# Sums stored tile by tile, and routing steps moved, in a fused attention and two-layer mixture-of-experts kernel

## The chip, the cores and the metric

The kernel runs on one core of one Trainium2 chip. Its engines are TensorE (PE: matmuls; PEld: its weight loads), VectorE (DVE), ScalarE (ACT), GpSimd (POOL) and SyncE (SP), with 16 DMA engines that move data between the chip's main memory (DRAM) and the core's on-chip memory (SBUF); PE writes its sums to PSUM. The metric is the device time of one execution in microseconds (us), as the median of three runs.

## The reference

Attention of 4 batches, 8 heads, 576 positions, 64 dimensions, in two steps over 32 packed queries, gives 2304 tokens of 512 numbers. A first mixture of experts takes all 4 experts for every token, weighted with given probabilities. A second takes, for every token, the two experts with the largest noisy logits out of 8:

```python
def _moe2_ref(x, w_gate, w_noise, noise, w1, w2):
    logits = x @ w_gate
    noise_scale = np.log1p(np.exp(x @ w_noise))
    noisy_logits = logits + noise_scale * noise
    top2 = np.argpartition(-noisy_logits, 2, axis=1)[:, :2]
    top2_l = np.take_along_axis(noisy_logits, top2, axis=1)
    top2_l = top2_l - top2_l.max(-1, keepdims=True)
    top2_w = np.exp(top2_l)
    top2_w /= top2_w.sum(-1, keepdims=True) + 1e-09
    out = np.zeros((N, D), dtype=np.float32)
    for e in range(E):
        for k in range(2):
            mask = top2[:, k] == e
            ...
            h = np.maximum(x[mask] @ w1[e], 0.0)
            out[mask] += top2_w[mask, k, None] * (h @ w2[e])
    return out.astype(np.float32)
```

N is 2304, D 512, F (the hidden width) 1024, and all numbers are float32.

## The kernel before

**Matmuls.** A float32 product is made of three matmuls of numbers split into a high and a low half (`mm3`, L64 to L67: high·high at L65, high·low and low·high at L66 and L67). The halves are made on arrival by ACT (high, L70) and by DVE or POOL (low, L71); for hidden values by L476 (ACT) and L477 (DVE).

**Stages.** Attention comes first, then the first mixture (MoE1), whose second matmul for the last block runs tile by tile (128 tokens each), five tiles of eight steps; places in this stretch are written `TM + 8*t + f` with TM = 200. Then comes the second mixture (MoE2); its places are `S2 + 8*j + f` with S2 = 300, where j counts blocks of work and f the eight steps of one.

**Blocks of MoE2.** An expert has room for 640 tokens, five tiles. The blocks in order are: tiles 0 to 2 of expert 0, tiles 0 to 2 of expert 1, tiles 3 and 4 of expert 0, tiles 3 and 4 of expert 1 (`EA` = 2 early experts, `tA` = 3 early tiles), and then experts 2 to 7 with all five tiles. A block is `e_mm1` (first matmul, hidden values to `gh`, `gl`) one step ahead of `e_mm2` (second matmul, sums in `acc`), and at the end of its last step `y_out` (L887, L889) writes each tile, times its weight, to `Y`.

**Routing.** Tokens are routed in four groups of tiles (`Route`): `ra` tiles 0 to 8, `rb` 9 to 12, `rc` 13 to 15, `rd` 16 and 17. `r1` (L548) stores a tile of x to `x2d` in DRAM and transposes it. `pos1` counts ranks with small matmuls of `utri` and `ones` (L628, L630, L633), `pos2` (DVE) makes the slots, `put` (L682, POOL) writes one record of 16 bytes per token and choice to `meta` in DRAM by an indirect DMA, `rest` (L701, L702) stores `sdd` and `gwd` for a fallback.

**Records and rows.** `mt_early` (L746) loads the records of the three early tiles of experts 0 and 1; `mt_index` (L759) casts them to integers `mti`, on POOL for the early ones. For the experts from 2 on (`mt_rest`, called in `mt_late`) it also runs 32 small matmuls on PE (L766) and makes an index `iq` of quarter rows (L768, DVE). `gather` fetches the rows `xg` of x from `x2d` (L811 whole rows for experts 0 and 1, L820 quarter rows for the others), `xg_t` turns them (L833 on PE for experts 0 and 1, by DVE for the others).

**Sums over the two experts of a token.** A token's lower expert leaves its part in `yd` in DRAM: `y_store` (L906) stores all five tiles of `Y[e]`, 1280 KB, once per expert, at the place `s + 8.13` of the block of work that ends it. `g_load` (L847) gathers the parts of earlier experts from `yd` into `gt` on POOL, after `g_zero` (L843, a memset). `y_out` or `y_add` (L894) adds them and `y_scatter` (L898, POOL) writes rows to the output; each row is written in the end by the token's higher expert.

**What sets the order.** Every engine works through its instructions in program order, and SP and POOL their DMA issues too. The order is written by hand: `at(place, f)` puts a step into a list, and `run(upto)`, called after every tile of matmuls, carries out the steps whose place has been reached, in the order of places. The weights (`raw`, 512 KB each, L132) are issued by SP in the same order, in three buffers; a load waits until its buffer has been split.

Of the kernel before, what the change touches and what calls it, by code (L numbers as in the profile page):

```python
# [15 lines left out]
OP = mybir.AluOpType  # L16
# [4 lines left out]
D, FF, E1, E2 = 512, 1024, 4, 8  # L21
# [9 lines left out]
def tile_pack_attn_moe_moe(ctx: ExitStack, tc: tile.TileContext, qT, kT, pT, vv, dp, noise,  # L31
                           w1, w2, m1, m2, wg, out, cap=CAP):
    nc = tc.nc
# [25 lines left out]
    yd = tc.dram_tile((NSLOT, D), F32, name="yd")  # L59
# [23 lines left out]
    cnt = consts.tile([128, 8], F32, name="cnt")  # L83
# [61 lines left out]
    def at(place, f, *a):  # L145
        fill.append((place, len(fill), f, a))
# [7 lines left out]
    TM, S2 = 200, 300  # L154
# [11 lines left out]
    for k in range(8):  # L166
        e = k % E1
# [6 lines left out]
    tA = T2 - T2 // 2  # L174

    EA = 2
    subs = [(e, 0, tA) for e in range(EA)] + [(e, tA, T2 - tA) for e in range(EA)] + [(e, 0, T2) for e in range(EA, E2)]
    vec, gps = nc.vector, nc.gpsimd
# [283 lines left out]
    for n, u in enumerate(at_u):  # L462
        s = 15 + 18 * n
# [4 lines left out]
        s = (50, 58)[n]  # L468
# [245 lines left out]
    ra, rb, rc, rd = Route(0, 9, aux_ps), Route(9, 4, acc_ps), Route(13, 3, mm_ps), Route(16, 2, mm_ps)  # L714
# [6 lines left out]
    for t in range(4):  # L721
        at(120.14 + t, rb.r1, t)
        at(121.13 + t, rb.r2, t)
    rb.tail([125.2, 126.1, 126.2, 127.1, 127.2, TM + 8.5, TM + 9.5], (TM + 10.2, 0.01))
    at(TM + 10.5, lambda: nc.vector.tensor_scalar(cnt[:, 0:EA], cnt[:, 0:EA], float(tA * 128), None, op0=OP.max))
    at(TM + 8, rc.begin)
    for t in range(3):
        at(TM + 8 * t + 9.4, rc.r1, t)
# [10 lines left out]
    XG, XT, Gt, H2, Y = {}, {}, {}, {}, {}  # L739
    mt_i = {}  # L740

    def mt_load(e0, e1, t0, t1):
        n = len(mt_i)
        m = rtp.tile([128, e1 - e0, t1 - t0, 4], F32, name="mt", tag=f"mt{n}", bufs=1)
        r0, r1 = e0 * cap + t0 * 128, (e1 - 1) * cap + t1 * 128
        ins = nc.sync.dma_start(m.rearrange("p e t c -> p (e t) c"),  # L746
                                meta[r0:r1, :].rearrange("(x p) c -> p x c", p=128))
        ix = rtp.tile([128, 3, e1 - e0, t1 - t0], I32, name="mti", tag=f"mti{n}", bufs=1)
        mt_i[n] = 0
        if t1 - t0 == T2:  # L750
            iq = rtp.tile([128, 4, (e1 - e0) * T2], I32, name="iq", tag=f"iq{n}", bufs=1)
            for e in range(e0, e1):
                IQ[e] = (iq, (e - e0) * T2)
            return m, ix, ins, iq
        return m, ix, ins
# [17 lines left out]
    def mt_w(e, t):  # L773
        m, _, a, b = MT[e, t]
        return m[:, a, b, 1:2]

    def mt_ix(e, t, i):
        _, ix, a, b = MT[e, t]
        return ix[:, i, a, b:b + 1]

    def mt_early(e):
        m, ix, ins = mt_load(e, e + 1, 0, tA)
        early_reads.append(ins)
        for t in range(tA):
            MT[e, t] = (m, ix, 0, t)
        at(TM + 26 + 0.1 * e, mt_index, m, ix, None, gps)

    def mt_late():
        for e in range(EA):
            m, ix, _ = mt_load(e, e + 1, tA, T2)  # L790
            at(S2 + 6.1, mt_index, m, ix)
            for t in range(tA, T2):
                MT[e, t] = (m, ix, 0, t - tA)
        mt_rest(EA, E2, S2 + 7.1)

    def mt_rest(e0, e1, place):
        m, ix, _, *quarters = mt_load(e0, e1, 0, T2)
        at(place, mt_index, m, ix, *quarters)
        for e in range(e0, e1):
            for t in range(T2):  # L800
                MT[e, t] = (m, ix, e - e0, t)
# [78 lines left out]
    def y_out(j, t):  # L880
        e, t0, n = subs[j]
        if t0 + t == 0:
            Y[e] = mo2.tile([128, T2, 512], F32, name="y", tag="y", bufs=2)
        y = Y[e][:, t0 + t, :]
        w = mt_w(e, t0 + t)
        if e == 0 or j < EA:
            nc.vector.tensor_scalar(y, acc2[t], w, None, op0=OP.mult)  # L887
        else:
            nc.vector.scalar_tensor_tensor(y, acc2[t], w, Gt[e][:, t0 + t, :], op0=OP.mult, op1=OP.add)  # L889
            y_scatter(e, t0 + t)  # L890

    def y_add(e, t):

        nc.vector.tensor_add(Y[e][:, t, :], Y[e][:, t, :], Gt[e][:, t, :])  # L894
        y_scatter(e, t)

    def y_scatter(e, t):
        ins = nc.gpsimd.indirect_dma_start(  # L898
            out=out, out_offset=bass.IndirectOffsetOnAxis(ap=mt_ix(e, t, 1), axis=0),
            in_=Y[e][:, t, :], in_offset=None, bounds_check=NTOK - 1, oob_is_err=False)  # L900
        for o in scat:
            tc.declare_no_dep(ins.ins, o.ins, reason="every token is written once")
        scat.append(ins)

    def y_store(e):
        nc.sync.dma_start(yd[e * cap:(e + 1) * cap, :].rearrange("(t p) d -> p t d", p=128), Y[e])  # L906

    n_over = []

# [10 lines left out]
        n_over.append(nc.values_load(n_over[0][0:1, 0:1], min_val=0, max_val=NTOK))  # L920

    for e in range(EA):
        at(TM + 21 + 0.1 * e, mt_early, e)
        at(TM + 26.5 + 0.1 * e, gather, e, range(tA - e))
    at(TM + 36.5, gather, 1, (tA - 1,))
    for t in range(tA):
        at(TM + 36 + t, xg_t, 0, t)
        at(S2 + 2.13 + t, xg_t, 1, t)
    at(S2 + 2.6, mt_late)
    at(S2 + 10.1, count_over)  # L930
    for j in range(EA, 2 * EA):
# [7 lines left out]
    for j in range(EA, len(subs)):  # L939
        s = S2 + 8 * j  # L940
        e = subs[j][0]
        if j + 1 < len(subs):
            at(s + 8.13, y_store, e)
        if e > 0:
            at(s + 2.14, g_zero, e)
            at(s + 3.14, g_load, e)
        if 0 < e < EA:
            for t in range(tA):
                at(s + 6.2 + 0.4 * t, y_add, e, t)
# [36 lines left out]
    for i in range(nj * NF):  # L986
        j, f = divmod(i, NF)
        n = subs[j][2]
        last = j == nj - 1
        if i + 1 < nj * NF:  # L990
            e_mm1(*divmod(i + 1, NF))
        if not (last and f == NF - 2):
            for t in range(n):
                if last and f == NF - 1:
                    e_mm2(j, f - 1, t)
                e_mm2(j, f, t)
                if f == NF - 1:
                    y_out(j, t)
                run(S2 + i + 0.1 * t + 0.09)
        run(S2 + i + 0.99)  # L1000
        if i == 8 * 3:
            load_over()
# [5 lines left out]
    with tc.If(rv > 0):  # L1008
        with tc.tile_pool(name="sl", bufs=2) as sl:
            with tc.For_i(0, NT, 1) as i:  # L1010
# [18 lines left out]
                r = sl.tile([128, 512], F32, name="sr")  # L1029
# [47 lines left out]
def build(arrays, cap=CAP):  # L1077
    import concourse.bacc as _bacc
    import concourse.tile as _tile
    from concourse import mybir as _mybir  # L1080

    nc = _bacc.Bacc("TRN2", target_bir_lowering=False, num_devices=1)
    args = []
    for name, a in arrays:
        args.append(nc.dram_tensor(f"in_{name}_dram", a.shape, _mybir.dt.from_np(a.dtype), kind="ExternalInput").ap())
    args.append(nc.dram_tensor("out_0_dram", (NTOK, D), F32, kind="ExternalOutput").ap())
    with _tile.TileContext(nc) as tc:
        tile_pack_attn_moe_moe(tc, *args, cap=cap)
    return nc
# [10 lines left out]
```

## Time and profile before

| | |
|---|---|
| three runs | 1213.94, 1215.02, 1222.16 us (median 1215.02) |
| the profiled execution | 1221.68 us, of which the span of the profile is 1219.4 us |
| PE busy | 1179.6 us, 97% of the span |
| DVE, ACT, POOL busy | 44%, 33%, 30% |
| granted TensorE clock, mean | 0.985 of full speed |
| stores of `Y` to `yd` | 7 of 1280 KB, by SP |
| weights `raw` of MoE2 and MoE1 | 80 and 32 loads of 512 KB, by SP |

The profile shows one execution, and its instructions add up to its own time, not to the median of the three. A wait is put down to what released it by the semaphores; "issue" means that the engine waited for nothing that the profile shows. The granted clock is a share of 2.4 GHz, so 0.50 is the lower of TensorE's two levels, 1.2 GHz. Matmuls are pipelined: one of 512 columns is shown with 0.39 us, and the next begins 0.23 us after it began.

### The profile page before, as it was taken

The page shows a single profiled execution, that of the slowest core. Times are in us where ns is not written, and L with a number is a line of the kernel's source. Part 1 is how long each engine was busy: PE and PEld are TensorE (multiplying, and loading weights), DVE is VectorE, ACT ScalarE, POOL GpSimd, SP SyncE. Part 2 cuts the span into 40 slices and gives each one's busy share as a digit, 9 for nine tenths or more (in the row PEclk, how much of TensorE's full clock was granted, in tenths as well). Part 3 has the DMA queues.
Part 4 walks back from the last instruction along what each step waited for, and adds up shares of the span by engine and source line. Part 5 has one row for each costly group of instructions (what it writes and reads, how often), then busy time and mean ns, then how long its engine had stood idle before and what let it go on. Part 6 is the DMA issues. An engine that isn't in the chain of part 4 may idle for free. (4 is left out here: it accounts for less than half of the span.)

```text
span 1219.4 us, 18289 instructions
## 1 busy us (share of the span) xinstructions
PE 1179.6 (97%) x7240; PEld 990.9 (81%) x7240; DVE 532.3 (44%) x1207; ACT 404.2 (33%) x856; POOL 369.0 (30%) x314
## 2 busy tenths in 40 slices
PE   6889999999999999999999989999998999999998
PEld 2668788788787888788888868799897888999997
DVE  5552242333445222533323546457553434445442
ACT  2442432332324334323223524334331323232321
POOL 0110200201203101115202144334576456476541
PEclk8999999999999999999999998999999898999999
DMA  7213033113141120210600237757534343545441
GB/s 293 101 50 134 19 105 117 35 35 130 36 142 44 57 100 18 82 40 19 113 28 1 70 103 134 143 162 235 170 109 132 116 134 118 170 127 169 134 165 41
DMA packets 53563, 126.00 MB, mean 103 GB/s; under 512 B 19242, under 2 KB 19642, under 8 KB 53472
## 3 DMA queue, kind: packets, MB, share of 16 engines
q1 hardware_dynamic: 42032, 104.66, 27.8%
q0 software_dynamic: 11440, 20.11, 5.5%
q8 instruction: 59, 0.97, 0.3%
q14 instruction: 32, 0.26, 0.1%
HBM read 110.33 MB, written 23.31 MB: 110 GB/s over the span
## 5 line engine op out<-in xcount | busy, mean ns | idle before, releaser
L71 POOL TENSOR_TENSOR w2l<-raw,w2h 128x1024 fp32r<-128x1024 f32 x32 | 76.6, 2394 | 401.8 <-ACT w2h L70 392.5
L65 PE MATMUL acc<-w2h,hh 128*128 128x512 f32 x448 | 183.3, 409 | 0.0
L67 PE MATMUL acc<-w2h,hl 128*128 128x512 f32 x448 | 177.8, 397 | 0.0
L66 PE MATMUL acc<-w2l,hh 128*128 128x512 f32 x448 | 176.7, 394 | 0.0
L477 DVE SCALAR_TENSOR_TENSOR hl<-mm,hh 128x224 fp32r<-128x224 f32 (+1 forms) x256 | 104.0, 423 | 147.0 <-ACT hh L476 146.3
L65 PE MATMUL mm<-xth,w1h 128*128 128x320 f32 (+2 forms) x512 | 160.1, 313 | 4.3 <-issue 4.1
L66 PE MATMUL mm<-xtl,w1h 128*128 128x320 f32 (+2 forms) x512 | 160.4, 313 | 3.3 <-issue 3.3
L67 PE MATMUL mm<-xth,w1l 128*128 128x320 f32 (+2 forms) x512 | 160.1, 313 | 0.3 <-issue 0.3
L65 PE MATMUL mm<-ath,mh 128*128 128x288 f32 x512 | 153.6, 300 | 5.5 <-ACT ath L70 2.6
L820 POOL DMA_INDIRECT xg<-x2d,iq x120 | 136.4, 1137 | 68.3 <-issue 33.1
L67 PE MATMUL mm<-ath,ml 128*128 128x288 f32 x512 | 151.4, 296 | 3.0 <-DVE ml L358 3.0
L66 PE MATMUL mm<-atl,mh 128*128 128x288 f32 x512 | 151.1, 295 | 0.5 <-DVE atl L71 0.4
L477 DVE SCALAR_TENSOR_TENSOR gl<-mm,gh 128x320 fp32r<-128x320 f32 (+2 forms) x128 | 62.7, 490 | 172.9 <-ACT gh L476 118.3
L476 ACT ACTIVATE hh<-mm 128x224 fp32r<-128x224 f32 (+1 forms) x256 | 93.1, 384 | 134.4 <-PE mm L67 104.6
L476 ACT ACTIVATE gh<-mm 128x320 fp32r<-128x320 f32 (+2 forms) x128 | 55.7, 436 | 234.9 <-PE mm L67 178.2
L65 PEld LDWEIGHTS acc<-w2h,hh 128*128 128x128 f32 x448 | 84.1, 188 | 44.0 <-issue 29.0
L65 PEld LDWEIGHTS mm<-ath,mh 128*128 128x128 f32 x512 | 96.1, 188 | 16.8 <-ACT ath L70 4.8
L65 PE MATMUL acc<-w2h,gh 128*128 128x512 f32 x272 | 108.9, 400 | 0.5 <-ACT xth L70 0.4
L67 PE MATMUL acc<-w2h,gl 128*128 128x512 f32 x272 | 107.4, 395 | 1.0 <-DVE gl L477 0.9
L66 PE MATMUL acc<-w2l,gh 128*128 128x512 f32 x272 | 108.0, 397 | 0.0
L66 PEld LDWEIGHTS mm<-xtl,w1h 128*128 128x128 f32 x512 | 97.6, 191 | 11.2 <-issue 7.7
L65 PEld LDWEIGHTS mm<-xth,w1h 128*128 128x128 f32 x512 | 97.6, 191 | 4.6 <-issue 1.4
(250 smaller groups left out, 1967.1 us busy)
## 6 DMA issues: line engine op xcount, KB each, us to landing
raw<-in_m_dram SPq DMA_DIRECT2D x80, 512.0 KB
raw<-in_w_dram SPq DMA_DIRECT2D x32, 512.0 KB
yd<-y SPq DMA_DIRECT2D x7, 1280.0 KB
w1h<-in_w_dram SPq DMA_DIRECT2D x16, 512.0 KB
w1l<-in_w_dram SPq DMA_DIRECT2D x16, 512.0 KB
v<-in_vv_dram SPq DMA_DIRECT2D x8, 640.0 KB
qk<-in_kT_dram SPq DMA_DIRECT2D x8, 576.0 KB
qk<-in_qT_dram SPq DMA_DIRECT2D x8, 576.0 KB
```

What stands on the lines that cost most here:

```text
L65: nc.tensor.matmul(o, ah, bh, start=start, stop=False)
L66: nc.tensor.matmul(o, ah, bl, start=False, stop=False)
L67: nc.tensor.matmul(o, al, bh, start=False, stop=stop)
L71: (eng or nc.vector).tensor_sub(l, x, h.bitcast(F32))
L476: nc.scalar.activation(hd, src, AF.Relu)
L477: nc.vector.scalar_tensor_tensor(ld, src, 0.0, hd.bitcast(F32), op0=OP.max, op1=OP.subtract)
L820: nc.gpsimd.indirect_dma_start(out=XG[j][t][:, b * 128:(b + 1) * 128], out_offset=None, in_=x2d.rearrange("t (q d) -> (t q) d", q=4), in_o ...
```

## The change

It has three parts. (a) `y_store` stores one tile (256 KB), directly after the tile has been written by `y_out` or summed by `y_add`; the store per expert goes. (b) `pos1`, `pos2`, the eight `put` and the `rest` of tiles 9 to 12 get earlier places, as do the loads of the early records, their casts and the gathers of the first two blocks of work; the place of expert 0's gathers now lies between the casts of the two experts. (c) The index of the experts from 2 on is placed two steps later.

```diff
-    rb.tail([125.2, 126.1, 126.2, 127.1, 127.2, TM + 8.5, TM + 9.5], (TM + 10.2, 0.01))
-    at(TM + 10.5, lambda: nc.vector.tensor_scalar(cnt[:, 0:EA], cnt[:, 0:EA], float(tA * 128), None, op0=OP.max))
+    rb.tail([125.2, 126.1, 126.2, 127.1, 127.2, TM + 7.2, TM + 8.0], (TM + 8.1, 0.01))
+    at(TM + 9.2, lambda: nc.vector.tensor_scalar(cnt[:, 0:EA], cnt[:, 0:EA], float(tA * 128), None, op0=OP.max))
...
-        at(TM + 26 + 0.1 * e, mt_index, m, ix, None, gps)
+        at(TM + 23 + 0.1 * e, mt_index, m, ix, None, gps)
...
-        mt_rest(EA, E2, S2 + 7.1)
+        mt_rest(EA, E2, S2 + 9.1)
...
         if e == 0 or j < EA:
             nc.vector.tensor_scalar(y, acc2[t], w, None, op0=OP.mult)
+            if e == 0:
+                y_store(e, t0 + t)
         else:
             nc.vector.scalar_tensor_tensor(y, acc2[t], w, Gt[e][:, t0 + t, :], op0=OP.mult, op1=OP.add)
             y_scatter(e, t0 + t)
+            if e + 1 < E2:
+                y_store(e, t0 + t)
...
         nc.vector.tensor_add(Y[e][:, t, :], Y[e][:, t, :], Gt[e][:, t, :])
         y_scatter(e, t)
+        y_store(e, t)
...
-    def y_store(e):
-        nc.sync.dma_start(yd[e * cap:(e + 1) * cap, :].rearrange("(t p) d -> p t d", p=128), Y[e])
+    def y_store(e, t):
+        r = e * cap + t * 128
+        nc.sync.dma_start(yd[r:r + 128, :], Y[e][:, t, :])
...
     for e in range(EA):
-        at(TM + 21 + 0.1 * e, mt_early, e)
-        at(TM + 26.5 + 0.1 * e, gather, e, range(tA - e))
+        at(TM + 18 + 0.1 * e, mt_early, e)
+        at(TM + 23.05 + 0.1 * e, gather, e, range(tA - e))
...
-        if j + 1 < len(subs):
-            at(s + 8.13, y_store, e)
```

On PE, in the second tile of the last block of MoE1: the order before, up to the first of the rank matmuls (`rb` is what they read, `lol`, `hh` and `hl` are hidden values of the tile).

```order
L67 MATMUL acc_6738<-w2h_6322,lol_6387 128x512
L65 MATMUL acc_6764<-w2h_6057,hh_6436 128x512
L66 MATMUL acc_6764<-w2l_6058,hh_6436 128x512
L67 MATMUL acc_6764<-w2h_6057,hl_6437 128x512
L65 MATMUL acc_6764<-w2h_6057,hh_6475 128x512
L66 MATMUL acc_6764<-w2l_6058,hh_6475 128x512
L67 MATMUL acc_6764<-w2h_6057,hl_6476 128x512
L628 LDWEIGHTS utri_84
L628 MATMUL mm_6772<-rb_6730,utri_84 128x32
```

And there in the changed kernel, from the same matmul on:

```order
L67 MATMUL acc_6738<-w2h_6322,lol_6387 128x512
L628 LDWEIGHTS utri_84
L628 MATMUL mm_6764<-rb_6730,utri_84 128x32
L630 LDWEIGHTS ones_85
L630 MATMUL mm_6764<-rb_6730,ones_85 128x24
```

The rank matmuls now stand six matmuls earlier, directly behind the last matmul of the tile before.

On POOL, from the eight `put` of tiles 9 to 12 to the first weights of experts: the difference, in which L759 are the casts of the early records and L811 the first gathers.

```order
 L682 DMA meta<-rr,rsi 5120x4 x8
-L759 CAST mti<-mt 128x3 x6
-L811 DMA xg<-x2d,mti 128x512 x5
+L759 CAST mti<-mt 128x3 x3
+L811 DMA xg<-x2d,mti 128x512 x3
+L759 CAST mti<-mt 128x3 x3
+L811 DMA xg<-x2d,mti 128x512 x2
 L71 TENSOR_TENSOR w2l<-raw,w2h 128x1024
```

The three casts and two gathers of expert 1 now stand behind the three gathers of expert 0; the `put` keep their place on POOL.

On PE, in the second block of MoE2's work (`gh`, `gl`: hidden values; `xth`: rows of x): the order before, around the 32 small matmuls of the index.

```order
L65 MATMUL acc_7243<-w2h_7265,gh_7529 128x512
L66 MATMUL acc_7243<-w2l_7266,gh_7529 128x512
L67 MATMUL acc_7243<-w2h_7265,gl_7530 128x512
L766 MATMUL mm_7604<-mt_7415,ident_79 32x30 x16
L65 MATMUL acc_7247<-w2h_7265,gh_7529 128x512
L66 MATMUL acc_7247<-w2l_7266,gh_7529 128x512
L67 MATMUL acc_7247<-w2h_7265,gl_7530 128x512
L65 MATMUL mm_7634<-xth_7391,w1h_7491 128x384
```

And in the changed kernel:

```order
L65 MATMUL acc_7635<-w2h_7442,gh_7614 128x512
L66 MATMUL acc_7635<-w2l_7443,gh_7614 128x512
L67 MATMUL acc_7635<-w2h_7442,gl_7615 128x512
L766 MATMUL mm_7673<-mt_7415,ident_79 32x30 x16
L65 MATMUL acc_7639<-w2h_7442,gh_7614 128x512
L66 MATMUL acc_7639<-w2l_7443,gh_7614 128x512
L67 MATMUL acc_7639<-w2h_7442,gl_7615 128x512
L65 MATMUL mm_7700<-xth_7391,w1h_7569 128x384
```

The small matmuls stand at the same spot of a step, two steps later, among other weights (`w2h_7442` in place of `w2h_7265`).

On SP, the loads of the records and of the weights keep their order around L766. The three stores of expert 0's first tiles now follow four loads of weights, with fifteen loads behind them; for the experts from 2 on two stores, one load and three stores follow each other. The store of x tile 13, which stood ahead of the `sdd` and `gwd` of tiles 9 to 12, now stands behind them.

## Rows read from the trace of the kernel before

**Rows 1.** Page, busy us of each engine, share of the span, instructions.
```profile
PE 1179.6 (97%) x7240; PEld 990.9 (81%) x7240; DVE 532.3 (44%) x1207; ACT 404.2 (33%) x856; POOL 369.0 (30%) x314
```

**Rows 2.** Waits of PE, 690 to 870 us: total us, times, longest us.
```profile
PE mm L833 <- DMA xg<-x2d,mti: 4.2, 1, 4.2
PE mm L766 <- DMA mt<-meta: 1.8, 1, 1.8
PE acc L67 <- DVE gl L477: 0.9, 2, 0.6
PE acc L65 <- ACT xth L70: 0.4, 1, 0.4
```

**Rows 3.** Waits of PE, 870 to 1220 us.
```profile
PE mm L65 <- issue: 4.1, 5, 1.5
```

**Rows 4.** Windows: us; PE, PEld, DVE, ACT, POOL busy; clock, DMA, GB/s.
```profile
929.51:936.45 6.94, 6.94 (x41) 6.33 (x39) 0.39 (x2) 0.44 (x1) 5.42 (x6) 1.00 0.73 238
936.45:952.50 16.05, 12.10 (x40) 9.20 (x39) 5.39 (x8) 3.83 (x6) 12.90 (x12) 0.68 0.33 100
1001.37:1015.67 14.30, 10.36 (x41) 8.14 (x39) 4.95 (x7) 3.92 (x7) 11.94 (x10) 0.76 0.27 77
```

**Rows 5.** Timeline, 701.5 to 703.4 us: start us, us, what [idle before <-releaser].
```profile
701.59 0.40 PE L67 MATMUL acc<-w2h,lol 128*128 128x512 f32 x1
...
702.98 0.19 DVE L620 TENSOR_TENSOR rb<-ro 128x32 bf16<-128x32 f32 x1
...
703.23 0.19 PE L628 MATMUL mm<-rb,utri 128*128 128x32 bf16 x1
```

**Rows 6.** Timeline of POOL, 696 to 745 us, and PE, 727 to 732.4.
```profile
707.08 0.99 POOL L682 DMA_INDIRECT meta<-rr,rsi  x1 [11.03 <-DVE ro L699]
...
724.07 0.44 POOL L759 CAST mti<-mt 128x3 int32<-128x3 f32 x3 [7.03 <-DMA mt<-meta]
724.79 0.43 POOL L759 CAST mti<-mt 128x3 int32<-128x3 f32 x3 [0.28 <-DMA mt<-meta]
725.76 1.06 POOL L811 DMA_INDIRECT xg<-x2d,mti  x1 [0.54 <-POOL mti L759]
...
731.92 0.63 PE L833 MATMUL mm<-ident,xg 128*128 128x128 f32 x4 [4.23 <-DMA xg<-x2d,mti]
```

**Rows 7.** Windows of half clock, columns as in rows 4.
```profile
780.50:783.90 3.40, 3.40 (x14) 3.12 (x11) 0.00 (x0) 0.46 (x1) 1.53 (x2) 0.50 0.92 354
732.00:739.00 7.00, 7.00 (x29) 6.14 (x30) 3.04 (x5) 2.74 (x4) 6.20 (x5) 0.55 0.70 198
```

**Rows 8.** Timeline of all engines, 776 to 788 us.
```profile
776.36 9.75 SPq L132 DMA_DIRECT2D raw<-in_m_dram  x4
...
779.89 0.64 PE L766 MATMUL mm<-mt,ident 128*32 128x30 f32 x32 [1.78 <-DMA mt<-meta]
...
783.44 1.06 ACT L70 ACTIVATE w1h<-raw 128x1024 fp32r<-128x1024 f32 x1 [8.98 <-DMA raw<-in_m_dram]
...
784.53 1.23 DVE L71 TENSOR_TENSOR w1l<-raw,w1h 128x1024 fp32r<-128x1024 f32 x1 [7.16 <-ACT w1h L70]
...
785.68 0.55 DVE L477 SCALAR_TENSOR_TENSOR gl<-mm,gh 128x384 fp32r<-128x384 f32 x1
...
786.28 0.49 PE L67 MATMUL acc<-w2h,gl 128*128 128x512 f32 x1 [0.62 <-DVE gl L477]
```

**Rows 9.** Timeline of SP's DMA issues, 924 to 990 us.
```profile
924.76 0.38 SPq L906 DMA_DIRECT2D yd<-y  x1
...
989.68 0.38 SPq L906 DMA_DIRECT2D yd<-y  x1
```

**Rows 10.** Page, DMA queues: packets, MB, share of 16 engines.
```profile
q8 instruction: 59, 0.97, 0.3%
```

**Rows 11.** Timeline of POOL, 870 to 930 us.
```profile
872.30 2.03 POOL L820 DMA_INDIRECT xg<-x2d,iq  x1 [0.30 <-issue]
...
927.75 1.04 POOL L820 DMA_INDIRECT xg<-x2d,iq  x1 [0.31 <-issue]
```

## The prediction

> **What bounds the kernel now.** I read the busy times of the page first. TensorE (PE) works in 1179.6 us, 97% of the span [rows 1], so only the remaining 3%, and what the clock takes, can be given back by moving work about. Next come the waits of PE in the second half of the span, where all the edits lie. Before 870 us two waits stand out: 4.2 us at L833 for the first gathered rows `xg`, and 1.8 us at L766 for the records `mt` [rows 2]. After 870 us PE waits for no other engine; its gaps there have "issue" as their releaser [rows 3]. Then I read the timeline around each place that the change touches, and the windows for the granted clock there.
>
> The profiled execution took 1221.68 us (span 1219.4, 2.3 around it). The three timed runs were 1213.94, 1215.02 and 1222.16. The profiled one is thus like the slowest of them, 6.66 above the median. The windows offer a reason. Two stretches after 930 us do the same 40 or 41 matmuls as the 6.94 us ahead of them, but take 16.05 and 14.30 us [rows 4]: 9.11 and 7.36 us more. I read the median as a run with one such stall fewer, about 8. I form the sum against 1221.68 and carry its difference over to 1215.02.
>
> **Positions of tiles 9 to 12 (`pos1` two steps earlier).** PE now meets L628 two matmul tiles earlier, that is six matmuls of 0.234 us (seven lie between 701.59 and 703.23 [rows 5]), or 1.40 us. It would get there at 701.83. But its operand `rb` is written by DVE from 702.98 to 703.17 [rows 5], so PE stands for 1.34 us, and the matmuls queued behind stand with it. Nothing comes earlier by this: the records still leave POOL from 707.08 [rows 6], when the rest of the slots' arithmetic on DVE is done. What PE loses is in front of a wait of 4.23 us whose end a DMA sets [rows 6], so it costs 0; if that cover went, 1.34.
>
> **Early records (`mt_early`, casts, gathers).** In the old order POOL casts the records of expert 0, then those of expert 1, then issues the first gather at 725.76 [rows 6]. In the new one the gathers of expert 0 stand ahead of the second cast. The first gather loses the 0.72 us from 724.07 to 724.79 that separate the casts [rows 6]; PE's wait ends that much earlier: −0.7. That the load itself is placed three steps earlier brings nothing, since the cast has waited 7.03 us for the records already [rows 6], whatever the place of their load. After the wait TensorE runs at half clock (1.2 of 2.4 GHz): 7.00 us at a granted 0.55 [rows 7], a loss of 3.15. A wait of 1.78 us [rows 8] is followed by 3.40 us at 0.50, a loss of 1.70 [rows 7]. Between these two, 0.59 us of clock hang on each us of waiting: −0.4 for 0.72. The bounds are −3.9 (wait and clock loss both as good as they can get: 0.72 + 3.15) and +0.7. The upper end comes from SP: the store of x tile 13 now stands behind `sdd` and `gwd`, where it is issued while the records are landing; its 256 KB take 0.74 us at the 354 GB/s of [rows 7]. I take −1.1, since the store is small beside the 7 us that the records need anyway.
>
> **Index of the third expert (`mt_index` two steps later).** The wait of 1.78 us at 779.89 goes [rows 8], and it looks like a gain of 1.8 plus 1.7 of clock. But I looked at what is late next. SP issued the weights `raw` at 776.36; ACT waited 8.98 us for them, until 783.44; DVE makes the low half from 784.53 and only then the `gl` at 785.68 for which PE waits until 786.28 [rows 8]. None of this hangs on L766, and SP's order of `mt` and `raw` stays. So 786.28 is a fixed date. PE goes on at 778.11 instead of 779.89, does the work sooner and waits some 4 us for the weights instead of 0.62. The gain is 0. The 32 small matmuls of L766 (0.64 us [rows 8]), which lay ahead of that date, come two steps later into a stretch in which PE has no gap: +0.6. The clock is the open part: the 3.40 us at 0.50 [rows 7] lay ahead of the fixed date and cost nothing; after the longer wait the half clock can reach beyond it, by anything from 0 to the 3.15 that follow the 4.23-us wait [rows 7]. I take 1.0, a third, as in the old order the clock fell 2.4 us after the wait began (778.11 to 780.50), so a good part of it should fall into the new wait. Together +1.6; bounds −3.5 (wait and clock, 1.78 + 1.70, both gained, if the weights come sooner) and +3.7 (0.6 + 3.15). The index itself comes two steps later, and with it the first gathers in quarters; these load rows for a block of work that starts three blocks on, so that delay is hidden.
>
> **Stores of the sums, tile by tile.** Seven stores of 1280 KB become 35 of 256 KB: 28 more issues on SP, which take 0.4 us each [rows 9] and lie on a queue that otherwise only issues weights. They wait for DVE's `y`, and behind them are the next weights; these wait for the release of their buffers anyway, so 0. At 854 PE waits 0.4 us for `xth` and 0.3 for a second `gl` (0.9 less the 0.62 above) [rows 2, 8], while the store shares the DMA engines with gathers. Two fifths of it now go out after the other three: −0.4; bounds −0.7 (both gone) and +0.4 (one more such wait).
>
> What of the two stalls [rows 4]? Each comes 11.7 us after a store, issued at 924.76 and 989.68 [rows 9], but the five other stores are followed by none. So I cost this at 0 in the forecast and make it a rival.
>
> The page's queue table shows 59 packets and 0.97 MB of instructions on q8 [rows 10], 16 KB each. The Trainium skill ("Runtime: NRT & Kernel Launch", section "Instruction fetch mechanics") says that instructions come in blocks of 16 KiB over a DMA queue of their own, the next page during the current one, and mostly hidden; the trace agrees on the size. By that rule the stores' bursts would not hold PE, splitting them would be worth nothing and the time would be 1215.1; if the bursts did hold the fetch, rival 1 applies.
>
> **Sum.** 0 − 1.1 + 1.6 − 0.4 = +0.1: 1221.8 by the profiled execution's own time, 1215.1 by the median. By the bounds, −3.9 − 3.5 − 0.7 = −8.1 to +0.7 + 3.7 + 0.4 = +4.8, so 1206.9 to 1219.8.
>
> **Rivals.** 1: the 1280-KB burst causes the stalls of PE that are put down to "issue", and splitting it removes them. For it: both come 12 us after such a store, with the DMA engines busy just before (0.73 at 238 GB/s) [rows 4]. Against it: five stores without a stall, and engines at only 0.33 and 0.27 of their capacity during it [rows 4]. Price: 1221.8 − 16.5 = 1205.3 from the profiled execution, 1215.1 − 8.2 = 1206.9 from the median with one stall; 1198.6 if the median run also held both.
>
> 2, on the slower side: the stalls come where the gathers follow the scatters too quickly. In the two periods with a stall the first gather in quarters took 1.04 us on POOL (927.75); in three without one it was held about twice as long, as for the 2.03 us at 872.30 [rows 11]. Split stores leave the queue sooner, so that the hold can go in the other periods as well. It decides from the point where such a first gather takes 1.04. Each further stall costs 8.2, the mean of the two: 1223.3 with one, 1231.5 with two. Against it: nothing shows that the gather's duration and the stall are cause and effect.
>
> A third, that an edit doesn't do what it says, is in the forecast already: `pos1` makes nothing earlier, and the index moves a wait instead of removing it.
>
> **How the numbers follow.** The forecast has 0.60, rival 1 0.27, rival 2 0.13. A measurement can tell about 1%, 12.2 us, from no change: 1202.9 to 1227.2. Below it lies only the case of rival 1 in which the median loses both stalls, a third of it: 0.09. Above it lies half of rival 2: 0.07. The rest, 0.84, is the same. The range of 1203 to 1224 takes in the forecast's own (1206.9 to 1219.8), two thirds of rival 1 and rival 2's single stall.
>
> **What would show it.** Right: the first L811 gather ahead of the second cast, PE's wait at L833 3.5 us; a wait of 1.3 us at L628; none at L766, but one of about 4 us for `gh` or `gl` near 781 to 785 with w1h on ACT again the last thing late; stalls by "issue" as before, some 7 to 9 us each. Wrong: no stall at all, in several executions, and a time near 1206 (rival 1); three or more stalls with first gathers of 1.04 us (rival 2); or the weights landing before 783.4, by which the wait of L766 would be a true gain of up to 3.5.

## The result, and the profile after

Timed 20 times each, the changed kernel takes 1237.78 us (median; 1221.35 to 1261.60), the kernel before 1218.40 us (1207.31 to 1227.93). The ratio is 1.0124, with a 95% interval of 1.0085 to 1.0163: the change makes the kernel slower by about 1.2%. (The ratio leaves out the slower executions, eight of the changed kernel's twenty among them; the two medians alone would give 1.016.) The forecast was no change, 1215.1 us, with a range up to 1224.

The profiled execution of the changed kernel has a span of 1236.6 us, 17.2 more than the one before. The page's busy times, to be held against [rows 1]:

```profile
PE 1183.6 (96%) x7240; PEld 994.1 (80%) x7240; DVE 534.5 (43%) x1207; ACT 404.5 (33%) x856; POOL 367.5 (30%) x314
```

PE does the same 7240 matmuls and is busy 4.0 us longer; the rest of the 17.2 us is idle time. The waits of PE from 690 to 870 us (total us, times, longest us) answer to [rows 2]:

```profile
PE acc L67 <- DVE gl L477: 2.5, 2, 1.9
PE mm L833 <- DMA xg<-x2d,mti: 2.3, 1, 2.3
PE acc L65 <- ACT gh L476: 1.8, 4, 0.7
PE mm L553 <- DVE x L533: 1.7, 1, 1.7
PE mm L628 <- DVE rb L620: 1.2, 1, 1.2
```

The waits for `xg` and `mt` together came from 6.0 down to 2.3 us, but waits for `gl`, `gh`, `x` and `rb` took their place. After 870 us, against [rows 3]:

```profile
PE mm L65 <- issue: 6.7, 6, 1.7
PE mm L66 <- issue: 4.7, 7, 1.6
PE mm L67 <- issue: 3.8, 5, 1.7
```

PE's time without a visible releaser ("issue") has doubled: 15.2 us here, where the kernel before had 7.7 in the same view (4.1 + 3.3 + 0.3). To see where, the stretch after 860 us is best cut into the steps of PE's work: each begins with the first matmul on `xth` and holds the 39 matmuls of one step of five tiles. An ordinary step takes 6.94 us. The windows of the changed kernel for one ordinary step and the four that took over 7.3 us (columns as in [rows 4]):

```profile
935.40:942.34 6.94, 6.94 (x40) 6.33 (x39) 0.00 (x0) 0.00 (x0) 5.42 (x6) 1.00 0.66 231
942.34:959.32 16.98, 11.27 (x40) 9.33 (x39) 3.19 (x5) 3.62 (x6) 13.77 (x13) 0.70 0.26 75
1014.84:1022.91 8.07, 7.52 (x40) 6.40 (x39) 4.38 (x8) 3.62 (x6) 7.00 (x6) 1.00 0.32 97
1064.70:1079.18 14.48, 9.74 (x40) 8.26 (x39) 4.60 (x7) 3.35 (x6) 12.19 (x10) 0.76 0.25 74
1127.76:1143.63 15.87, 11.15 (x41) 8.76 (x39) 4.95 (x7) 4.02 (x7) 12.99 (x11) 0.78 0.27 73
```

Three steps take 14.5 to 17.0 us, and a fourth 8.07. The kernel before had two long ones [rows 4]. Below, a step of over 13 us is called a long step. Beyond 6.94 each, these steps hold 10.0 + 1.1 + 7.5 + 8.9 = 27.6 us (from the unrounded rows), against 16.5 before: 11.2 more. Of the other 6.0 us, 2.4 lie ahead of all edits (`rb` is written at 705.38 in place of 702.98), and 3.5 between there and the first of these steps (from `rb` it is 233.5 us to 936.45 before, 237.0 to 942.34 now).

What happens in a long step is seen one engine further. The timeline of an ordinary step and of the first long one, for matmuls that end a half's sums in PSUM, and for ACT and DVE ("remote" means that the profile names no instruction behind the semaphore event that ended the wait):

```profile
930.07 0.31 PE L67 MATMUL mm<-xth,w1l 128*128 128x320 f32 x1
...
930.48 0.44 ACT L476 ACTIVATE gh<-mm 128x320 fp32r<-128x320 f32 x1 [3.85 <-PE mm L67]
...
938.77 0.31 PE L67 MATMUL mm<-xth,w1l 128*128 128x320 f32 x1
...
945.74 0.44 ACT L476 ACTIVATE gh<-mm 128x320 fp32r<-128x320 f32 x1 [11.90 <-remote]
...
946.21 0.49 DVE L477 SCALAR_TENSOR_TENSOR gl<-mm,gh 128x320 fp32r<-128x320 f32 x1 [11.12 <-ACT gh L476]
...
952.06 0.44 ACT L476 ACTIVATE gh<-mm 128x320 fp32r<-128x320 f32 x1 [5.88 <-remote]
```

The last matmul of the second half of `mm` starts at 938.77, the first half's at 937.01; PE then goes on with `acc`. ACT is idle and starts the first half's `gh` only at 945.74, after 11.90 us without work, and the second half's at 952.06, 13 us after its matmuls; DVE follows ACT at once (0.47 us). In an ordinary step `gh` starts within half a microsecond of the start of its last matmul, as at 930.48. So it is not PE that is late first: what PE has issued reaches ACT late, and PE, still running at 942, then crawls. Whether the sums are written late or only announced late these rows don't tell, since the ends of matmuls are modelled. The granted clock (0.70 to 0.78 in the three long steps) falls after PE has begun to idle and adds its part: in this step PE's first gap begins at 942.64, and the clock is 1.00 until 946 and 0.50 from 947 to 956.

The early records, against [rows 5] and [rows 6]:

```profile
705.38 0.19 DVE L620 TENSOR_TENSOR rb<-ro 128x32 bf16<-128x32 f32 x1
...
705.62 0.18 PE L628 MATMUL mm<-rb,utri 128*128 128x32 bf16 x1 [1.23 <-DVE rb L620]
...
709.50 0.99 POOL L682 DMA_INDIRECT meta<-rr,rsi  x1 [11.04 <-DVE ro L699]
```

then, 18 us later, the records on POOL:

```profile
727.95 0.44 POOL L759 CAST mti<-mt 128x3 int32<-128x3 f32 x3 [8.51 <-DMA mt<-meta]
728.95 1.06 POOL L811 DMA_INDIRECT xg<-x2d,mti  x1 [0.56 <-POOL mti L759]
```

and PE at the first rows of x:

```profile
735.14 0.45 PE L833 MATMUL mm<-ident,xg 128*128 128x128 f32 x1 [2.30 <-DMA xg<-x2d,mti]
```

All of this starts 2.40 us later than before, so times are read from `rb`: the first `put` 4.12 us behind it (4.10 before), the cast 22.57 (21.09), the first gather 23.57 (22.78), PE's restart 29.76 (28.94).

### The profile page after: what moved, and what is told of

Its sections match the earlier page's. It is cut to its first block, busy times and chain, and to the rows that moved or that the text cites. A ratio compares the mean times of both kernels' runs of the same rounds, so it can differ in the third digit from the quotient of the medians.

```text
span 1236.6 us, 18338 instructions
## 1 busy us (share of the span) xinstructions
PE 1183.6 (96%) x7240; PEld 994.1 (80%) x7240; DVE 534.5 (43%) x1207; ACT 404.5 (33%) x856; POOL 367.5 (30%) x314
## 4 chain that ended last, share of the span: by engine, by line
PE 82%; issue 6%; DVE 5%; DMA 3%; ACT 2%; POOL 1%; SPq 0%; POOLq 0%; DVEq 0%; ACTq 0%
PE acc L65 13%; PE acc L67 13%; PE acc L66 13%; PE mm L65 11%; PE mm L67 10%; PE mm L66 10%; PE mm L351 2%; PE accx L66 2%; PE accx L65 2%; PE accx L67 2%; DMA meta<-rr,rsi 1%; PE mm L833 0%; PE mm L562 0%; DVE ta L313 0%; DMA xg<-x2d,mti 0%
## 5 line engine op out<-in xcount | busy, mean ns | idle before, releaser
L71 POOL TENSOR_TENSOR w2l<-raw,w2h 128x1024 fp32r<-128x1024 f32 x32 | 76.6, 2394 | 404.2 <-ACT w2h L70 395.0
L820 POOL DMA_INDIRECT xg<-x2d,iq x120 | 133.4, 1112 | 67.4 <-issue 33.1
```

The costliest lines, as they stand in the source:

```text
L71: (eng or nc.vector).tensor_sub(l, x, h.bitcast(F32))
L820: nc.gpsimd.indirect_dma_start(out=XG[j][t][:, b * 128:(b + 1) * 128], out_offset=None, in_=x2d.rearrange("t (q d) -> (t q) d", q=4), in_o ...
```

## Experiments

Five chips were used in turn, one for each group of runs, and the kernel before was timed beside every group on the same chip. It took 1203 to 1236 us on them, so ratios count, not times. It was not profiled there, so its long steps are read from the traces of kernels that keep its stores. "Long steps" are counted in the one trace of each kernel. The ratio of store5_2 rests on three executions, those of after_again and a_brk2 on four, that of a_only on five, the others on seven to twelve; one execution of b_only that took 4085.03 us is not counted.

| kernel | chip | before, us | ratio, 95% interval | long steps |
|---|---|---|---|---|
| a_only | 1 | 1233.08 | 1.0121 (1.0057 to 1.0185) | 5 |
| b_only | 1 | 1233.08 | 0.9987 (0.9954 to 1.0020) | 2 |
| c_only | 1 | 1233.08 | 1.0006 (0.9972 to 1.0040) | 2 |
| b_c | 1 | 1233.08 | 1.0007 (0.9973 to 1.0041) | 2 |
| before_brk | 2 | 1203.22 | 1.0010 (0.9997 to 1.0022) | 0 |
| a_brk | 2 | 1203.22 | 1.0012 (0.9999 to 1.0025) | 0 |
| before_zero | 2 | 1203.22 | 1.0006 (0.9992 to 1.0021) | 0 |
| store5 | 2 | 1203.22 | 0.9997 (0.9983 to 1.0010) | 0 |
| after_again | 3 | 1235.86 | 1.0125 (1.0043 to 1.0206) | 4 |
| before_brk2 | 3 | 1235.86 | 0.9936 (0.9889 to 0.9983) | 2 |
| a_brk2 | 3 | 1235.86 | 1.0199 (1.0144 to 1.0255) | 4 |
| store5_2 | 3 | 1235.86 | 1.0145 (1.0066 to 1.0223) | 4 |
| s5_45 | 4 | 1206.02 | 1.0002 (0.9987 to 1.0016) | 0 |
| s5_23 | 4 | 1206.02 | 1.0004 (0.9989 to 1.0019) | 0 |
| store_late | 4 | 1206.02 | 1.0001 (0.9986 to 1.0015) | 0 |
| store2 | 4 | 1206.02 | 0.9987 (0.9973 to 1.0000) | 0 |
| mix1 | 5 | 1235.86 | 0.9963 (0.9930 to 0.9997) | 3 |
| mix2 | 5 | 1235.86 | 1.0000 (0.9954 to 1.0047) | 3 |

### Which part costs it: a_only, b_only, c_only, b_c

Each is the kernel before with a part of the change: the stores alone; the places of routing and early records alone; the place of the index alone; the last two together, that is, the changed kernel with one store per expert.

```diff
a_only:  the store of one tile, as in the change; nothing else
b_only:  rb.tail(... TM + 7.2, TM + 8.0], (TM + 8.1, 0.01)), TM + 9.2, TM + 18, TM + 23, TM + 23.05
c_only:
-        mt_rest(EA, E2, S2 + 7.1)
+        mt_rest(EA, E2, S2 + 9.1)
b_c:     b_only and c_only
```

> Only the stores change: one of 256 KB per tile, the rest as before. Theory 1 (the tile-by-tile stores bring on further stalls of PE while the quarter rows are gathered): 8 to 15 us slower than before, 1.007 to 1.012, and three or more of the five periods with a stretch in which the first hidden values (gh) come over 4 us after their matmuls. Theory 2 (the moved routing and index cost it): within 2 us of before, and stalls in two periods as before.

> Only the routing of tiles 9 to 12 and the early records move. Theory 1: +1 to +2 us (the matmuls ahead of L833 lose more than the gather gains), 1.001. Theory 2: at least half of the 15 us, 1.006 or more.

> Only the index of the experts from 2 on comes two steps later. Theory 1: +1 us, 1.001, with PE waiting for gl or gh around 785 in place of mt. Theory 2: at least half of the 15 us, 1.006 or more, since the later first gather of quarter rows shifts all later ones.

> The changed kernel with one store of 1280 KB per expert, as before. Theory 1: +2 to +4 us, 1.002 to 1.003, the sum of the two parts; the rest of the loss goes. Theory 2: as slow as the changed kernel, 1.012.

The stores alone cost 1.0121, as much as the whole change; the other parts, one by one or together, cost nothing that can be told from zero. Theory 2 falls. The long steps of b_c (windows, columns as in [rows 4]; the third row is the longest step besides):

```profile
940.42:955.57 15.15, 10.73 (x41) 8.20 (x40) 4.91 (x7) 3.53 (x6) 12.55 (x11) 0.77 0.26 76
1004.15:1019.56 15.41, 11.69 (x41) 8.52 (x40) 4.95 (x7) 3.92 (x7) 12.64 (x11) 0.78 0.27 79
1096.70:1106.83 10.13, 8.72 (x39) 8.03 (x40) 6.03 (x9) 4.06 (x7) 0.35 (x1) 0.83 0.20 61
```

and those of a_only:

```profile
942.09:957.06 14.97, 10.89 (x41) 8.80 (x39) 4.98 (x8) 4.17 (x7) 12.37 (x11) 0.77 0.28 79
1006.32:1021.93 15.61, 11.98 (x39) 9.37 (x40) 4.95 (x7) 4.17 (x7) 12.76 (x11) 0.67 0.26 76
1071.15:1086.78 15.63, 12.25 (x39) 9.28 (x40) 4.96 (x8) 4.16 (x7) 12.76 (x11) 0.67 0.27 77
1128.42:1141.62 13.20, 8.73 (x40) 6.37 (x39) 0.86 (x1) 0.00 (x0) 10.16 (x11) 0.89 0.53 192
1153.40:1168.63 15.23, 10.86 (x40) 8.25 (x39) 6.28 (x10) 4.81 (x8) 6.00 (x7) 0.78 0.34 100
```

With one store per expert there are two, after experts 2 and 3, as before; with one per tile they come in four periods of gathers, after experts 2 to 5, and in the last of them PE is hardly out of one when it is in the next. (The five of the table and the rows are those over 13 us; one of 11.78 lies between the last two.)

c_only also shows the mechanism foretold for the index. Its timeline where L766 stood:

```profile
781.92 1.06 ACT L70 ACTIVATE w1h<-raw 128x1024 fp32r<-128x1024 f32 x1 [8.58 <-DMA raw<-in_m_dram]
...
783.40 0.50 PE L65 MATMUL acc<-w2h,gh 128*128 128x512 f32 x1 [3.08 <-ACT gh L476]
```

The wait for `mt` is gone, and PE waits 3.08 us for `gh` instead, behind a `w1h` for whose weights ACT had waited 8.58 us.

### Do breaks on POOL help: before_brk, a_brk, before_zero, and the number of stores: store5

Theory A came from the rows of POOL: in the long steps of before and after it issues DMAs one after the other, and PE's last gap ended 1.3 to 2.3 us after POOL had started the memset of `gt`.

```diff
before_brk, a_brk (in gather, behind the four quarter gathers of a tile; a_brk with the stores of a_only):
+            nc.gpsimd.memset(brk, 0.0)
before_zero:
-            at(s + 2.14, g_zero, e)
+            at(s + 0.5, g_zero, e)
store5 (y_store(e, t) as in the change):
-            at(s + 8.13, y_store, e)
+            for t in range(T2):
+                at(s + 8.13, y_store, e, t)
```

> The kernel before, with a small POOL memset (64 numbers a row) behind the four quarter gathers of every tile. Theory A (POOL's unbroken row of DMA issues holds up the semaphores between PE and ACT until POOL does something else): no long stall is left, gh at most 1 to 2 us after its matmuls, 10 to 17 us faster than before, 0.986 to 0.992. Theory B (the transfers themselves, stores and scatters and gathers together, hold PE up): two long stalls as before, 1.000.

> Stores tile by tile alone, with the same small memset behind the gathers of every tile. Theory A: the four long stalls go, and the kernel is as fast as before_brk. Theory B: four long stalls, 1.010 or more.

> The kernel before, with the memset of gt (2.25 us on POOL) directly behind the first tile's four gathers, where it stood behind the third tile's: 12 gathers follow it without a break. Theory A: the stalls are cut short or move behind the memset; within 8 us of before either way. Theory B: two stalls as before, 1.000.

> Five stores of 256 KB per expert, all at the place of the one store of 1280 KB. If the number of the stores brings on the further stalls (each a transfer and a semaphore more for SP): four long stalls and 1.010 as with a_only. If their earlier place does (bytes in flight while the scatters and first gathers go out): two long stalls, 1.000.

These told nothing of the theories, but much else: on this chip none of the four has a single step over 7.3 us after 862 us, the kernel before takes 1203.22 us, and all four are within 0.2% of it. Stores tile by tile (with the memsets) took 1.0012 here (0.9999 to 1.0025), five stores 0.9997. Without long steps, then, no cost of the stores can be told from zero.

### The same on a chip with long steps: after_again, before_brk2, a_brk2, store5_2

> The changed kernel once more, beside the next three on one chip. Theory A (long stalls, more of them with stores tile by tile): where the kernel before shows the long stalls, 1.010 to 1.016 of it; on a chip on which it shows none, at most 3 us slower, 1.000 to 1.003. Theory C (the loss has another cause): 1.010 or more on any chip.

> The kernel before with the small POOL memset behind the four quarter gathers of every tile, again. Theory A, where the kernel before shows long stalls: they are gone or shorter than 3 us each, 0.986 to 0.994. Theory B (transfers): two long stalls, 1.000. On a chip without stalls 1.001, as in the first run.

> Stores tile by tile with the same memsets, again. Theory A, where there are long stalls: as fast as before_brk2. Theory B: four long stalls, 1.010 or more. On a chip without stalls 1.001.

> Five stores of 256 KB at the place of the one store, again. Where there are long stalls: 1.010 if the number of stores counts, 1.000 if their earlier place does. On a chip without stalls 1.000.

The changed kernel loses its 1.0125 again. Theory A falls, as far as short breaks go: with the memsets behind every tile's gathers the four long steps are there as without (a_brk2, 1.0199), and the kernel before keeps its two (before_brk2; its ratio of 0.9936 is not explained by them). The five stores at the place of the old one decide the other question. The long steps of store5_2:

```profile
938.28:953.81 15.53, 11.66 (x41) 8.67 (x39) 5.08 (x8) 4.16 (x7) 12.63 (x12) 0.78 0.28 81
1002.41:1018.43 16.02, 12.37 (x41) 9.13 (x39) 5.27 (x8) 4.17 (x7) 13.12 (x12) 0.68 0.30 80
1067.62:1083.19 15.57, 11.77 (x39) 9.21 (x39) 5.42 (x8) 4.16 (x7) 12.67 (x12) 0.67 0.27 80
1132.38:1148.16 15.78, 12.14 (x39) 9.38 (x39) 5.33 (x8) 4.17 (x7) 12.88 (x11) 0.68 0.28 81
```

Four again, and 1.0145. So neither the earlier place of the stores nor the bytes are needed for the loss; five issues where there was one are enough. By which way they act is not shown by this.

### Which store a long step hangs on: s5_45, s5_23, store_late, store2

```diff
s5_45 (s5_23: e in (2, 3)), in y_store:
+        if e in (4, 5):
+            for t in range(T2):
+                r = e * cap + t * 128
+                nc.sync.dma_start(yd[r:r + 128, :], Y[e][:, t, :])
+            return
store_late:
-            at(s + 8.13, y_store, e)
+            at(s + (11.0 if e > 1 else 8.13), y_store, e)
store2, in y_store: two stores, of tiles 0 to 2 and of tiles 3 and 4
```

> One store of 1280 KB per expert as before, but five of 256 KB for experts 4 and 5 alone, in whose wake the kernel before shows no long stall. Theory D (a long stall follows a store by how that one expert's sums are stored): long stalls after the stores of experts 2, 3, 4 and 5, 1.010 to 1.014. Theory E (the count of transfers or the time up to there decides): two, after experts 2 and 3, or none besides; 1.000. On a chip without stalls 1.000.

> Five stores for experts 2 and 3 alone, where the kernel before has its long stalls anyway. Theory D: the same two long stalls, 1.000. Theory E: further long stalls after experts 4 and 5, 1.010 or more. On a chip without stalls 1.000.

> One store per expert, but for the experts from 2 on three steps later (some 20 us), behind the 12 gathers of quarter rows. Theory F (a store in flight while scatters and first gathers go out is what starts a long stall): none in the two periods, 10 to 17 us faster than before, 0.986 to 0.992, and gh in time. Theory G (the gathers alone do it): two long stalls, 1.000. On a chip without stalls 1.000.

> Two stores per expert (768 and 512 KB) at the place of the one. If the number counts: three or four long stalls, 1.005 to 1.014. If only single tiles do it: two, 1.000. On a chip without stalls 1.000.

This chip, too, showed no long step in any of the four, and no difference (0.9987 to 1.0004). The questions stayed open. It does confirm that no form of the stores costs anything measurable where long steps don't occur.

### Expert by expert: mix1, mix2

```diff
mix1 (mix2: e == 3 and e == 5):
+        if e == 4:
+            for t in range(T2):
...
-            at(s + 8.13, y_store, e)
+            at(s + (11.0 if e == 2 else 8.13), y_store, e)
```

> One store per expert as before, except that expert 2's comes three steps later and expert 4's is five of 256 KB. On a chip with long stalls, theory D (each stall hangs on the store just ahead of it): a long stall after expert 3 and one after expert 4; none after expert 2 if the store's overlap with scatters and gathers starts it (theory F), one if the gathers alone do (theory G); about 1.000. Theory E (a count over the program): the stalls do not move with the expert whose stores are changed. On a chip without stalls 1.000 and nothing is told apart.

> One store per expert as before, except that expert 3's comes three steps later and expert 5's is five of 256 KB. On a chip with long stalls, theory D: one after expert 2 and one after expert 5; none after expert 3 by theory F, one by theory G; none after expert 4; about 1.000. Theory E: the same places as in mix1. On a chip without stalls 1.000 and nothing is told apart.

This chip has long steps. Those of mix1:

```profile
939.80:954.31 14.51, 10.63 (x41) 8.22 (x39) 4.56 (x7) 3.53 (x6) 11.91 (x11) 0.76 0.30 94
1002.89:1018.23 15.34, 10.70 (x41) 8.66 (x39) 4.94 (x7) 4.01 (x7) 12.57 (x11) 0.78 0.28 78
1067.70:1082.99 15.29, 11.97 (x41) 9.32 (x39) 5.16 (x8) 4.17 (x7) 12.66 (x11) 0.67 0.27 78
```

They follow experts 2, 3 and 4 (stores at 933.36, 991.20 and from 1051.35); none follows expert 5, with its single store. Of mix2, with the undisturbed stretch at 990 between:

```profile
935.94:951.24 15.30, 11.06 (x41) 8.62 (x39) 4.95 (x7) 4.09 (x7) 12.39 (x12) 0.78 0.27 80
990.00:999.00 9.00, 9.00 (x50) 8.03 (x49) 3.69 (x5) 2.86 (x5) 7.17 (x7) 1.00 0.67 222
1057.32:1073.33 16.01, 11.40 (x41) 9.23 (x40) 5.11 (x8) 3.83 (x6) 13.11 (x12) 0.68 0.27 83
1122.51:1138.31 15.80, 12.08 (x40) 9.34 (x41) 5.41 (x8) 4.16 (x7) 12.90 (x12) 0.68 0.28 83
```

They follow experts 2, 4 and 5 (stores at 924.25, 1045.62 and from 1106.44); none follows expert 3, whose store came at 992.70, behind the start of the gathers. Five stores were followed by a long step both times, at places where the kernel before had none, and the places moved with the expert whose stores were changed: this speaks for theory D and against E, on one trace each. But expert 4's single store is followed by one in mix2 and by none in the profile of before; a single store can go either way, so the form of the store doesn't decide alone. Theory F and G stay open: the late store brought no long step after expert 3, yet one after expert 2, where the gathers had begun at 931.10, ahead of the store at 933.36.

## Why the prediction was wrong

**The step that failed** is the one on the stores: that 28 more issues on SP cost 0, leave the stalls as they were, and gain 0.4 us. On their own the stores took the kernel to 1.0121, some 15 us. The stalls were looked at, and costed at 0 in the forecast, because five of the seven stores were followed by none. What the runs showed in its place: the stalls are long steps in which ACT gets PE's results late, by 4.5 to 13.3 us in the changed kernel's three; with one store per expert they come after experts 2 and 3, with five per expert after experts 2 to 5 (in the changed kernel's own two traces the step after expert 3 stayed at 8.07 and 8.80). How five issues bring them on stays open.

**Rival 2** had the direction and the price (8.2 us for each further stall; the three here hold 7.5 to 10.0), to which the prediction gave a chance of 0.13. One further stall was put at 1223.3 and two at 1231.5; the changed kernel's trace has one long step and a step of 8.07 more, the other traces with stores by tile two or three more. Its mark, a first gather of 1.04 us where it had been held for 2.0, was met in all five periods of the changed kernel, though in the first of them, after expert 1, with no long step ([rows 11] for before; the timeline of POOL):

```profile
878.19 1.04 POOL L820 DMA_INDIRECT xg<-x2d,iq  x1 [0.30 <-issue]
...
933.63 1.05 POOL L820 DMA_INDIRECT xg<-x2d,iq  x1 [0.30 <-issue]
...
999.22 1.04 POOL L820 DMA_INDIRECT xg<-x2d,iq  x1 [0.30 <-issue]
...
1055.99 1.04 POOL L820 DMA_INDIRECT xg<-x2d,iq  x1 [0.30 <-issue]
...
1119.07 1.05 POOL L820 DMA_INDIRECT xg<-x2d,iq  x1 [0.30 <-issue]
```

Its cause is another than was thought, though. The hold had nothing to do with scatters that drain. DVE's subtraction for the low half of weights in the kernel before:

```profile
872.18 1.23 DVE L71 TENSOR_TENSOR w2l<-raw,w2h 128x1024 fp32r<-128x1024 f32 x1 [0.46 <-ACT w2h L70]
...
928.33 1.23 DVE L71 TENSOR_TENSOR w2l<-raw,w2h 128x1024 fp32r<-128x1024 f32 x1 [0.45 <-ACT w2h L70]
```

At 872.18 it starts just ahead of the gather of 872.30, and that takes until 874.33, one ordinary microsecond after DVE is done (873.41); at 928.33 it starts behind the gather of 927.75, which isn't held. And the mark doesn't decide alone. On the second chip a_brk has it in every period, as here,

```profile
928.74 1.04 POOL L821 DMA_INDIRECT xg<-x2d,iq  x1 [0.31 <-issue]
```

and PE runs through the step at full pace:

```profile
928.62:935.56 6.94, 6.94 (x40) 6.33 (x40) 2.21 (x3) 2.13 (x4) 5.44 (x7) 1.00 0.82 297
```

On the chips with long steps, though, every period after experts 2 to 5 that has the mark holds a long or a lengthened step (in the 12 traces from such chips, 34 of 36 have a step of over 14 us; the two others, both of the changed kernel after expert 3, have 8.07 and 8.80), and of the 12 periods in which the first gather was held none holds a step over 10.2. The period after expert 3 in mix2 is one of these, at the start of the undisturbed stretch shown above, and that after expert 4, with its single store and its long step, is one of the others:

```profile
991.12 2.09 POOL L820 DMA_INDIRECT xg<-x2d,iq  x1 [0.30 <-issue]
...
1048.61 1.05 POOL L820 DMA_INDIRECT xg<-x2d,iq  x1 [0.30 <-issue]
```

So in mix1 and mix2 the mark sorts all eight periods, and the form of the store does not. Of the 22 periods with five stores all have it, of the 24 with one store at the old place 13. Five stores may thus act only by shifting the gathers against DVE's subtraction: a rival that no run here tells apart. Whether the held gather prevents the long step, or both follow from the same delay, wasn't tried.

**Rival 1** (the burst of one 1280-KB store causes the stalls, and splitting removes them) is refuted: with split stores there are more. Nor does the trace bear out that bursts hold the fetch of instructions: in the changed kernel's first long step, 942.34 to 959.32, these are all the DMA queues that moved anything (columns as in [rows 10]), q8 not among them, and it is missing in the two others too.

```profile
q0 software_dynamic: 385, 0.74, 15.5%
q1 hardware_dynamic: 144, 0.52, 10.2%
```

**Positions of tiles 9 to 12** went as worked out: PE stands 1.23 us at L628 (1.34 forecast), and the first `put` follows `rb` by 4.12 us in place of 4.10. (The 1.34 that the prediction names for a lost cover is not in its upper bound of +4.8; nothing hung on it here.)

**Early records**: the order on POOL is as foretold, but the term has the wrong sign in this trace. The gather was to come 0.72 us earlier and came 0.79 later from `rb`, since the cast, which lost its rival, waited 8.51 us for its records instead of 7.03. That is 1.48 us more, twice the 0.74 that the store of x tile 13 was given as a bound; that this store alone does it wasn't shown. The other traces with this part agree in sign: the cast waits 7.47 us in b_only, 7.67 in b_c and 7.50 in after_again, and PE restarts 28.93, 29.15 and 29.19 us behind `rb`, at best 0.01 ahead of the 28.94 of before. The wait at L833 shrank to 2.3 us as PE itself arrived later. By b_only (0.9987) none of it can be told from zero in the time.

**Index of the third expert**: the mechanism was right. There is no wait at L766, but one for `gh` or `gl` behind the weights in its place. Its size varies: some 4 us were foretold, c_only has 3.08 for `gh` and b_c 2.49, the changed kernel's own trace only 0.40, with 0.62 for `gl` behind it. Of the time, +1.6 us were forecast and c_only has +0.7 (1.0006 of 1233.08), with an interval of some 4 us on either side, so the term can't be told from zero.

**The base**: 1218.40 us over 20 runs of before, 1215.02 over the first three. How the profiled execution stood to the median was read as one stall more or less; over the five chips of the experiments the kernel before has medians from 1203.22 to 1235.86, so the chip, or the session on it, as each was used once, matters more than any of these edits.

What stays open is why ACT gets PE's sums late, why on some chips only, and why five stores bring it on where one may not. A lack of short breaks on POOL was shown not to be the reason, and neither the earlier place of the split stores nor their bytes are needed for the loss. Not tried was to shift the gathers against DVE's work with the stores left whole.

No version here beats the kernel before beyond doubt: before_brk2 does on one chip (0.9936) and before_brk, the same kernel, doesn't on another (1.0010); mix1 has 0.9963 and mix2, much like it, 1.0000.

## What to carry to other kernels

A transfer that is hidden by every row of the trace can still cost: splitting one store into five added no bytes and no wait that the profile names, and cost 1.2 to 1.5% on the chips with long steps, nothing measurable on the two others. Where a trace already shows stalls that nothing explains, an edit to the traffic just ahead of them should not be costed at zero; their number can change, and the price of one more can be read from the trace. And a gain or loss of 1% is worth timing on more than one chip before it is believed.

## What the runs showed of the hardware

The time of one program differs from chip to chip: the kernel before took 1203.22 and 1206.02 us on two chips, on which no trace shows a long step, and 1233.08, 1235.86 and 1235.86 on the three others, on which all do. Each chip was used in one session, so chip and session are not told apart. Sums can reach the next engine late though it is idle: 13 us between the last matmul at 938.77 and `gh` at 952.06, and DVE behind ACT is served at once. An indirect DMA that POOL starts while DVE subtracts two 128x1024 tiles is held until DVE is done: 2.03 us instead of 1.04. In all 20 traces together, 664 of the 672 that start in such a subtraction, at least 0.3 us before its end, end 0.8 to 0.9 us behind it, and none of the 3364 that start clear of DVE's L71 takes over 1.23 us.
